# Batch 0 of a linear-attention kernel: value scaling on GpSimd, numerator scaled in PSUM and divided on VectorE, in a reshuffled order

## The chip, the core and the metric

The kernel runs on one core of a Trainium2 chip. A core has five engines that run side by side, each with its own queue of instructions that it takes strictly in order: PE (TensorE, matmuls, results only into PSUM), DVE (VectorE), ACT (ScalarE), POOL (GpSimd, works on SBUF alone in this kernel) and SP (SyncE, which issues DMAs). Semaphores let an instruction wait for another engine. The metric is the device time of one execution in microseconds (us). The kernel before took 360.67 us, the median of three runs from 360.47 to 360.85.

## The reference

```python
# q, k, v: (8 batches, 8 heads, 576 tokens, 64), w_phi: (64, 128)
def phi(x):
    proj = x @ w_phi
    proj = proj - max(abs(proj), axis=-1)
    return concatenate([exp(proj), exp(-proj)], axis=-1)   # 256 features
q_p, k_p = phi(q), phi(k)
kv  = einsum('bhsf,bhsd->bhfd', k_p, v);  z = sum over s of k_p
num = einsum('bhsf,bhfd->bhsd', q_p, kv); den = einsum('bhsf,bhf->bhs', q_p, z) + 1e-6
x = (num / den) as (4608 tokens, 512)
out = (relu(x @ w_gate) * (x @ w_val)) @ w_out             # 512 -> 1536 -> 512
```

## The kernel before, in words

There are two halves: the attention of eight batches, and the feed-forward network (FFN) on their 4608 tokens. Each batch gives 512 tokens in four blocks of 128 (`i` = 0 to 3), and the last 64 tokens of two batches are handled together. FFN work of earlier batches stands between the steps of later ones, so that PE always has something to do, except at the start, where there is no earlier batch.

The order of everything is written out by hand in the string `ORDER`. Each word is one step: a name, its arguments, the PSUM banks after a colon, the SBUF buffers after an `@`. The words are emitted one after the other, and each engine gets its own instructions in that order. Nothing else sets the order; waits come from the data and from the reuse of banks and buffers. The steps that matter here, with their arguments (batch, head group `j` or `g`, block `i`, sign `s`):

- `zz.n` (L455): n matmuls on zeros, which fill PE's time at the start. `kf`, `kg`, `kh` (L645, L654): transpose the first keys. `k3` (L668): projects keys. `wd` (L431): turns `w_phi` into bf16 as soon as its DMA has landed.
- `ke` (ACT L688), `kx` (DVE L696): exponential of the projected keys, and their largest absolute value. `kk` (ACT L705): the factor `ek` per token that undoes the maximum. `kp` (ACT L716): the same, but into PSUM.
- `vs` (POOL L745): v times `ek`, one sign of a head group each; `vo` (POOL L757): the column of `ek` that makes the denominator; `vq` (POOL L773): the same for the leftover 64 tokens. For head group 0 (two heads) of batch 0, and its leftover tokens, DVE does this from PSUM instead: `vd` (L726), `vp` (L735), `vz` (L678).
- `kv` (PE L794): the sum over tokens, for head groups of 2, 3 and 3 heads; each needs its `vs` and the leftover tokens' `vr`. `kc` on ACT or `kd` on DVE (L805) copies it out.
- `qb` (PE L840), `qe` (ACT L869), `qx` (DVE L877), `qy`, `qz`, `qu`, `qw`: the same for q, ending in a scale `cq` for the negative sign.
- `nu` (PE L917): both signs' numerators, side by side in a bank. `nt` (DVE L938) scales the negative sign into `t`, `nv` (DVE L948) adds the positive one into `u`, `nr` (DVE L956) takes the reciprocal of the denominator, `nx` (POOL L960) divides into `xu`.
- `xp`, `xa` (PE L997, ACT L1011): transpose `xu` of batch 0, which `pv` and `pg` (PE L1224), batch 0's part of the FFN input, then read. Later batches use `xt`, a DMA.
- `lk`, `lq`, `lm`, `wl` (POOL) and `lw`, `lv` (SP): loads, where POOL and SP issue the DMAs. `fv`, `fg`, `fi`, `fo`, `fw`: FFN matmuls. `va` (ACT L1112) or `vb` (DVE L1115) copies a value tile out of PSUM, `ga` (DVE L1118) multiplies it in. `ps` (POOL L1337): sums that some `fw` matmuls read.

Of the kernel before, what the change touches and what calls it, by code (L numbers as in the profile page):

```python
# [16 lines left out]
ms.0 lf lm.0.0 ms.4@vr0 ms.6 id lk.0.2 lk.0.0 wq ms.3@vr1 if ms.5 zz.15:0 kf.0:1 ms.9 kf.1:2 zz.6:3  # L17
wd kh.0:1@kT0 sl k3.1.0:45 ke.0.1.0.0:4@kp0 w1:6 kg.1:2 kx.0.1.1:5@mk0 kx.0.1.0:4 wa:6 zz.2:7
k3.1.1:01 ke.0.1.3.0:1 lm.0.1 kx.0.1.2:0 zz.3:3 k0.2:2 lq.0.1 ke.0.1.3.1:1 k1.2:2@kT1 ke.0.1.0.1:4
zz.3:7 k0.0:6 ke.0.1.2.1:0 ke.0.1.1.1:5 k3.2.1:37 ke.0.1.2.0:0 kx.0.1.3:1 ms.2 lw.0.0 lw.0.1  # L20
k1.0:6@kT2 zz.5:4 k3.0.1:21 kk.0.1.0@ek0 k3.0.0:04 ke.0.1.1.0:5 ke.0.0.3.0:1@kp1 q0.1:5 lq.0.0
kx.0.2.3:7@mk1 kx.0.2.2:3 kk.0.1.1 ke.0.2.2.0:3@kp2 kx.0.0.0:0@mk2 kx.0.0.2:2 lv.0.1 ke.0.2.2.1:3
ke.0.0.1.1:4 kx.0.0.3:1 q1.1:5@qT0 ke.0.0.1.0:4 ke.0.0.3.1:1 lv.0.0 zz.6:6 q0.0:6 kx.0.0.1:4 wl.0.1
zz.4:3 k3.2.0:31 lv.0.2 ke.0.2.3.0:7 ke.0.0.2.1:2 ke.0.0.0.1:0 q1.0:6@qT1 ke.0.2.3.1:7 kx.0.2.1:1
zz.1:5 qb.1.1:5 zz.3:4 qb.0.1:4 kx.0.2.0:3 ke.0.0.0.0:0 zz.2:7 qb.0.0:0 qx.0.0.1:4 ke.0.0.2.0:2
zz.1:6 qb.1.0:2 qx.0.1.1:5 zz.7:7 qy.0.1:6 kp.0.0.0:0 ke.0.2.0.0:3 lk.1.3 kk.0.2.1@ek1 kp.0.0.1:0
kk.0.2.0 ke.0.2.1.1:1 vo.1@vs0 qx.0.1.0:2 qe.0.0.1.0:4@qp0 ke.0.2.0.1:3 qe.0.0.1.1:4 lq.1.2
qe.0.1.0.0:2@qp1 qe.0.1.0.1:2 vs.0.1.0 qz.0.1:6@my0 zz.4:7 qb.0.3:7 qx.0.0.0:0 zz.2:6 qy.0.0:3
vd.0.0.0:0@vs1 qz.0.0:3@my1 vs.0.1.1 qe.0.1.1.1:5 vp.0:0 qu.0.1@mz0 ke.0.2.1.0:1 qe.0.1.1.0:5 wl.0.0
vz.0:0 qb.0.2:6 zz.2:4 qb.1.3:3 zz.2:4 qb.1.2:2 vd.0.0.1:0 qu.0.0@mz1 vz.1:0 qe.0.1.3.0:3@qp2  # L30
vo.2@vs2 qw.0.0@cq0 qx.0.0.3:7 qx.0.0.2:6 qe.0.0.0.0:0 vs.0.2.1 zz.7:4 kv.0.0:1 qx.0.1.3:3 lw.1.1
vs.0.2.0 kc.0.0:1@kv0 kt.1.1@kT3 qe.0.0.0.1:0 kv.0.2:5 kv.0.1:4 qe.0.0.2.1:6@qp3 lm.1.1 kc.0.2:5
wl.1.1 kc.0.1:4 nu.0.0.0:1 nt.0.0.0:1@t0 zz.1:0 nu.0.0.2:5 qw.0.1 qx.0.1.2:2 qe.0.0.2.0:6
qe.0.1.3.1:3 nu.0.0.1:0 nv.0.0.0:1@u0 zz.2:4 nu.0.1.2:4 lv.1.2 nu.0.1.0:6 qe.0.1.2.1:2 nt.0.0.1:0@t1
lm.1.0 nt.0.0.2:5@t2 qy.0.2:1 nv.0.0.1:0 qe.0.0.3.0:7 nv.0.0.2:5 nt.0.1.0:6@t3 zz.2:3 nu.0.1.1:3
qy.0.3:0 nr.0.0@r0 qe.0.1.2.0:2 qz.0.2:1@my2 nv.0.1.0:6@u1 qz.0.3:0@my0 qu.0.2@mz2 zz.5:5
kr.1.1:1265 qe.0.0.3.1:7 nt.0.1.2:4@t0 nt.0.1.1:3@t1 qw.0.2 wl.1.0 nu.0.2.2:0 nx.0.0@xu0 nv.0.1.2:4
xp.0.0:7 nv.0.1.1:3 nt.0.2.2:0@t2 ke.1.1.3.1:5@kp3 nr.0.1@r1 nu.0.2.1:4 xa.0.0:7 nt.0.2.1:4@t3
nu.0.2.0:3 ke.1.1.0.1:1 nt.0.2.0:3@t0 qu.0.3@mz1 ke.1.1.0.0:1 pv.1.0:7 nv.0.2.1:4@u2 nv.0.2.2:0
nv.0.2.0:3 nu.0.3.1:4 qw.0.3 ke.1.1.1.0:2 nx.0.1@xu1 kx.1.1.0:1@mk3 xp.0.1:0 pa.1.0:7@val0  # L40
# [246 lines left out]
def kernel(  # L287
# [700 lines left out]
    def xT_cols(b, i):  # L988
        return xT(b)[:, :, P * i : P * (i + 1)]
# [488 lines left out]
```

## Time and profile before

| | |
|---|---|
| median of the runs | 360.67 us |
| the profiled execution itself | 360.87 us |
| span of its instructions | 359.1 us |
| busy: PE, POOL, DVE, ACT | 352.9, 325.6, 312.9, 235.8 us |

The span runs from the first to the last instruction; 1.77 us of the execution's 360.87 lie outside of it. Matmuls are pipelined, so the end of one lies after the start of the next; what PE spends on a step is best read from the starts. A row of a timeline has start, length, engine, line, operation, output and inputs, how many instructions were merged, and in brackets how long the engine had been idle and who released it. A row of the groups by form ends in the summed busy time, the mean of one in ns, and the idle time before them.

### The profile page before, as it was taken

How to read it: one execution, taken by the hardware profiler on the slowest of the kernel's cores; microseconds unless marked ns; L12 is line 12 of the kernel's file. 1: busy time of each engine (PE TensorE's matmuls, PEld its weight loads, DVE VectorE, ACT ScalarE, POOL GpSimd, SP SyncE). 2: the span in 40 equal slices, each digit the busy share in tenths (PEclk: the TensorE clock that was granted, in tenths of full speed). 3: DMA queues.
4: the chain of work that ended last, by engine and by line, in shares of the span. 5: the costliest groups of instructions: out<-in, count | busy, mean ns of one | idle time of the engine just before them, and what ended most of it. 6: DMA issues, size and time to landing. Idle time of an engine off the chain costs nothing.

```text
span 359.1 us, 10076 instructions
## 1 busy us (share of the span) xinstructions
PE 352.9 (98%) x3876; PEld 222.2 (62%) x3876; DVE 312.9 (87%) x721; ACT 235.8 (66%) x564; POOL 325.6 (91%) x393
## 2 busy tenths in 40 slices
PE   8999999999999999999999999999999999999996
PEld 6678966445575656765576546666656566444684
DVE  5999999989999999999997999999898853898744
ACT  3999996986698869786897269656861424454310
POOL 8674988999999999976999589989999999999994
PEclk9999999999999999999999999999999999999999
DMA  7999999990947494369215980778300221600017
GB/s 124 257 198 204 164 199 159 180 164 7 178 68 157 53 157 95 68 127 135 58 39 105 158 136 2 176 107 103 62 0 16 45 59 25 227 0 2 0 31 206
DMA packets 90770, 38.16 MB, mean 106 GB/s; under 512 B 64226, under 2 KB 86370, under 8 KB 90722
## 3 DMA queue, kind: packets, MB, share of 16 engines
q0 software_dynamic: 33504, 15.03, 32.5%
q1 hardware_dynamic: 56754, 21.83, 27.7%
q10 hardware_dynamic: 464, 0.66, 0.8%
q8 instruction: 30, 0.49, 0.6%
q14 instruction: 18, 0.15, 0.1%
HBM read 37.81 MB, written 9.44 MB: 132 GB/s over the span
## 4 chain that ended last, share of the span: by engine, by line
PE 85%; DVE 8%; ACT 2%; DMA 2%; issue 1%; POOL 1%; SPq 0%; DVEq 0%
PE bank L1097 35%; PE bank L1361 18%; PE bank L1194 10%; PE bank L794 5%; PE bank L1224 4%; PE bank L917 3%; PE bank L592 2%; PE bank L854 2%; PE bank L1256 2%; ACT kp L688 2%; DMA w64f<-in_w_phi_dram 2%; DVE t L938 1%; DVE u L948 1%; DVE h L1118 1%; DVE mk L696 1%
## 5 line engine op out<-in xcount | busy, mean ns | idle before, releaser
L688 ACT ACTIVATE kp<-bank 128x384 bf16<-128x384 f32 x192 | 84.2, 513 | 16.6 <-DVE mk L696 7.4
L1097 PE MATMUL bank<-xTs,wv 128*128 128x512 bf16 x304 | 75.7, 379 | 0.0
L1097 PE MATMUL bank<-xTs,wg 128*128 128x512 bf16 x304 | 74.6, 379 | 0.0
L869 ACT ACTIVATE qp<-bank 128x512 bf16<-128x512 f32 x128 | 69.9, 627 | 6.5 <-PE bank L854 4.2
L1118 DVE SCALAR_TENSOR_TENSOR h<-bank,val 128x512 bf16<-128x512 f32 x90 | 60.5, 680 | 6.7 <-PE bank L1097 4.5
L1112 ACT CAST val<-bank 128x512 bf16<-128x512 f32 x59 | 35.1, 594 | 33.4 <-PE bank L1097 30.4
L745 POOL TENSOR_TENSOR vs<-vn,ek 128x780 bf16<-128x780 f32 (+2 forms) x40 | 53.8, 1366 | 0.8 <-ACT ek L705 0.4
L696 DVE TENSOR_REDUCE mk<-bank 128x3 f32<-128x384 f32 x96 | 49.1, 542 | 0.2
L960 POOL TENSOR_TENSOR xu<-u,r 128x512 bf16<-128x512 f32 x36 | 37.4, 1045 | 11.6 <-DVE r L956 11.5
L1361 PEld LDWEIGHTS <-h 128*128 128x128 bf16 x432 | 41.1, 98 | 10.0 <-issue 2.6
L1097 PEld LDWEIGHTS <-wg 128*128 128x128 bf16 x304 | 27.8, 98 | 30.2 <-issue 1.3
L1097 PEld LDWEIGHTS <-wv 128*128 128x128 bf16 x304 | 27.6, 98 | 27.3 <-issue 0.9
L877 DVE TRANSPOSE_TENSOR_REDUCE maxq<-bank 128x16 f32<-128x512 f32 x56 | 36.9, 690 | 0.1
L948 DVE TENSOR_TENSOR u<-bank,t 128x195 f32<-128x195 f32 (+1 forms) x108 | 32.9, 327 | 1.8 <-POOL xu L960 0.9
L1361 PE MATMUL bank<-wo,h 128*128 128x256 bf16 x260 | 32.5, 273 | 0.0
L1337 POOL TENSOR_TENSOR vs<-h 128x256 bf16<-128x256 bf16 x42 | 28.0, 671 | 3.7 <-DVE h L1118 3.6
L938 DVE TENSOR_TENSOR t<-bank,cq 128x195 f32<-128x195 f32 (+1 forms) x96 | 29.6, 326 | 1.9 <-PE bank L917 1.2
L917 PEld LDWEIGHTS <-qp 128*128 128x128 bf16 x512 | 23.1, 98 | 10.2 <-issue 0.5
L1337 POOL TENSOR_TENSOR h<-h,vs 128x256 bf16<-128x256 bf16 x44 | 28.6, 676 | 0.0
L1337 POOL TENSOR_TENSOR vs<-vs,h 128x256 bf16<-128x256 bf16 x42 | 28.0, 672 | 0.6
L1337 POOL TENSOR_TENSOR h<-h 128x256 bf16<-128x256 bf16 x42 | 27.9, 674 | 0.3
L917 PE MATMUL bank<-kv,qp 128*128 128x65 bf16 x512 | 26.0, 193 | 0.2 <-ACT kv L805 0.2
(156 smaller groups left out, 686.0 us busy)
## 6 DMA issues: line engine op xcount, KB each, us to landing
vn<-in_v_dram SPq DMA_DIRECT2D x24, 256.0 KB, 4.3
out_dram<-xTs SPq DMA_DIRECT2D x17, 256.0 KB, 3.0
kn<-in_k_dram POOLq DMA_DIRECT2D x7, 512.0 KB, 8.1
qn<-in_q_dram POOLq DMA_DIRECT2D x7, 512.0 KB, 8.0
out_dram<-obp SPq DMA_DIRECT2D x14, 256.0 KB, 2.6
wv<-in_moe_w_val_dram POOLq DMA_DIRECT2D x3, 512.0 KB, 9.4
wg<-in_moe_w_gate_dram POOLq DMA_DIRECT2D x3, 512.0 KB, 8.8
wo<-in_moe_w_out_dram POOLq DMA_DIRECT2D x3, 512.0 KB, 8.3
```

The source lines that it names most:

```text
L688: nc.scalar.activation(kp_of(3 * b + j)[:, i, s].rearrange("p n f -> p (n f)"), bank[bk[0]][:, 0 : 3 * F], AF.Exp, scale=(1.0, -1.0)[s],)
L696: nc.vector.tensor_reduce(mk_of(3 * b + j)[:, :, i], bank[bk[0]][:, 0 : 3 * F].rearrange("p (n f) -> p n f", f=F), axis=AX.X, op=ALU.max, ...
L745: nc.gpsimd.tensor_tensor(vs_of(3 * b + j)[:, s, 0:n].rearrange("p n i e -> p (n i) e")[:, :, 0:e], src[:, lo:hi].rearrange("p h i e -> p ...
L869: nc.scalar.activation(qp_of(4 * b + i)[:, s, 4 * hq : 4 * hq + 4].rearrange("p h m -> p (h m)"), bank[bk[0]], AF.Exp, scale=(1.0, -1.0)[s],)
L877: nc.vector.tensor_reduce((maxq0[:, i] if b == 0 else maxq)[:, :, i, 4 * hq : 4 * hq + 4].rearrange("p t h -> p h t"), bank[bk[0]].rearran ...
L917: nc.tensor.matmul(bank[bk[0]][:, E * n : E * (n + 1)], lhsT=qp_of(4 * b + i)[:, s, h, :], rhs=kv_of(b)[:, h, s, 0:E],)
L948: nc.vector.tensor_tensor(u_of(serial(b, i))[:, lo:hi], parts(bk, n)[:, :, 0], t_of(3 * serial(b, i) + g)[:, 0:n], op=ALU.add,)
L960: eng.tensor_tensor(xu_of(n).rearrange("p (h d) -> p h d", d=D), u_of(n)[:, :, 0:D], r_of(n).to_broadcast([P, H, D]), op=ALU.mult,)
L1097: nc.tensor.matmul(bank[bk[0]], lhsT=w[:, dc, P * f : P * f + P], rhs=xT(g)[:, dc, :], start=(dc == 0), stop=(dc == NDC - 1),)
L1118: nc.vector.scalar_tensor_tensor(h2_of(g, f), bank[bk[0]], 0.0, val_of(NFC * g + f), op0=ALU.max, op1=ALU.mult)
L1337: eng.tensor_tensor(sum_of(g, n, j), a, b, op=op)
L1361: nc.tensor.matmul(bank[bk[0]][:, col : col + HN], lhsT=x[:, P * u : P * (u + 1)], rhs=w, start=(n in (1, 5, 6) and u == us[0] and j == 0) ...
```

## The change

In batch 0, and only there, two pieces of arithmetic move:

- The scaling of v of head group 0 and of the leftover tokens goes from DVE to POOL: two `kp`, two `vd`, one `vp` and two `vz` are gone, and two `kk`, two `vs`, one `vo` and two `vq` are new. POOL now scales all v.
- The numerator is made in halves of four heads. `bu` with s = 1 puts the negative sign into a bank; `bt` (DVE) scales it there, in PSUM; `bu` with s = 0 adds the positive sign onto it; `br` (DVE) takes the reciprocal of the denominators, and `bx` (DVE) divides into `xu`. 12 `nu`, 12 `nt`, 12 `nv`, 4 `nr` and 4 `nx` (POOL) are gone; 16 `bu`, 8 `bt`, 8 `br` and 8 `bx` are new.

Besides, single copies change engine: of the value tiles, 13 go from DVE to ACT and 8 from ACT to DVE; of the `kv` copies five go from ACT to DVE and one back; one transposed block goes from DVE to ACT and one output block from ACT to DVE. And the whole of `ORDER` is shuffled in small steps. PE has 64 matmuls of the numerator before and after, and 85 matmuls on zeros.

```diff
+    HALVES = ((0, 4), (4, 8))
+    def do_bu(bk, b, i, g, s):
+        lo, hi = HALVES[g]
+        for h in range(lo, hi):
+            n = h - lo
+            nc.tensor.matmul(
+                bank[bk[0]][:, E * n : E * (n + 1)],
+                lhsT=qp_of(4 * b + i)[:, s, h, :],
+                rhs=kv_of(b)[:, h, s, 0:E],
+                start=(s == 1 and h == lo),
+                stop=(h == hi - 1),
+                skip_group_check=(s == 0),
+            )
+    def part(bk, g):
+        lo, hi = HALVES[g]
+        return bank[bk[0]][:, 0 : E * (hi - lo)].rearrange("p (h e) -> p h e", e=E)
+    def do_bt(bk, b, i, g):
+        lo, hi = HALVES[g]
+        nc.vector.tensor_tensor(
+            part(bk, g),
+            part(bk, g),
+            scales(b, i)[:, lo:hi][:, :, None].to_broadcast([P, hi - lo, E]),
+            op=ALU.mult,
+        )
+    def do_br(bk, b, i, g):
+        lo, hi = HALVES[g]
+        nc.vector.reciprocal(r_of(serial(b, i))[:, lo:hi], part(bk, g)[:, :, D : D + 1])
+    def do_bx(bk, b, i, g):
+        n, (lo, hi) = serial(b, i), HALVES[g]
+        nc.vector.tensor_tensor(
+            xu_of(n).rearrange("p (h d) -> p h d", d=D)[:, lo:hi],
+            part(bk, g)[:, :, 0:D],
+            r_of(n)[:, lo:hi].to_broadcast([P, hi - lo, D]),
+            op=ALU.mult,
+        )
...
 ORDER = """
-ms.0 lf lm.0.0 ms.4@vr0 ms.6 id lk.0.2 lk.0.0 wq ms.3@vr1 if ms.5 zz.15:0 kf.0:1 ms.9 kf.1:2 zz.6:3
-wd kh.0:1@kT0 sl k3.1.0:45 ke.0.1.0.0:4@kp0 w1:6 kg.1:2 kx.0.1.1:5@mk0 kx.0.1.0:4 wa:6 zz.2:7
...
+ms.0 lf lm.0.0 ms.4@vr0 ms.6 id lk.0.2 lk.0.0 wq ms.3@vr1 if ms.5 zz.15:0 kf.0:1 kf.1:2 zz.2:3
+zz.5:4 sl kg.1:2@kT0 kh.0:1 zz.6:5 wd k3.1.0:67 kx.0.1.1:7@mk0 k3.1.1:03 zz.3:1 kx.0.1.2:0
```

Three places show what the new order does to single engines. The first is PE and ACT at the very start, in the lines of `ORDER` above: ahead of the first key projection `k3.1.0` stood `zz.6`, and now stand `zz.2`, `zz.5` and `zz.6`, thirteen matmuls on zeros where six were. ACT's first exponential was `ke.0.1.0.0`, which reads what `k3.1.0` wrote; it is now `ke.0.1.3.0`, which reads what `k3.1.1` writes. On ACT the two `kk.0.1` stood behind 7 and 9 of batch 0's `ke` and are now both behind 12 `ke` and `wa`.

The second place is POOL's queue before the first `kv`, first in the kernel before. `vs_97` and `vs_99` are the scaled v of head groups 1 and 2 (12 is 3 heads by 4), `kn`, `qn` the loads of batch 1's k and q, `wv` and `wg` thirds of the FFN's weights.

```order
L464 DMA kn_71<-in_k_dram 128x8x256
L757 CAST vs_97<-ek_91 128x24
L496 DMA qn_73<-in_q_dram 128x8x256
L745 TENSOR_TENSOR vs_97<-vn_75,ek_91 128x12x64 x2
L558 DMA wv<-in_moe_w_val_dram 128x4x512
L757 CAST vs_99<-ek_92 128x24
L745 TENSOR_TENSOR vs_99<-vn_75,ek_92 128x12x64 x2
```

And the same stretch of POOL's queue after the change, where `vs_98` is head group 0 and `vr_103` the leftover tokens:

```order
L465 DMA kn_71<-in_k_dram 128x8x256
L746 TENSOR_TENSOR vs_97<-vn_75,ek_91 128x12x64 x2
L497 DMA qn_73<-in_q_dram 128x8x256
L746 TENSOR_TENSOR vs_98<-vn_75,ek_92 128x8x64
L758 CAST vs_98<-ek_92 128x2x8
L746 TENSOR_TENSOR vs_98<-vn_75,ek_92 128x8x64
L774 TENSOR_TENSOR vr_103<-vm_76,ek_92 64x8x65
L746 TENSOR_TENSOR vs_99<-vn_75,ek_93 128x12x64
L758 CAST vs_97<-ek_91 128x24
L774 TENSOR_TENSOR vr_103<-vm_76,ek_92 64x8x65
L758 CAST vs_99<-ek_93 128x24
L746 TENSOR_TENSOR vs_99<-vn_75,ek_93 128x12x64
```

Five instructions for head group 0 and the leftover tokens now stand among those of groups 1 and 2, and the load of `wv`, which stood between `vs_97` and `vs_99`, stands behind all of them.

The third place is DVE at batch 0's first numerators, in the kernel before (`my` and `h` belong to q's maxima):

```order
L938 TENSOR_TENSOR t_123<-bank_64,cq_115 128x130
L877 TENSOR_REDUCE h_152<-bank_65 128x4x4
L948 TENSOR_TENSOR u_127<-bank_64,t_123 128x130
L938 TENSOR_TENSOR t_124<-bank_63,cq_115 128x195
L938 TENSOR_TENSOR t_125<-bank_68,cq_115 128x195
L948 TENSOR_TENSOR u_127<-bank_63,t_124 128x195
L948 TENSOR_TENSOR u_127<-bank_68,t_125 128x195
L938 TENSOR_TENSOR t_126<-bank_69,cq_115 128x130
L956 RECIPROCAL r_130<-u_127 128x8
```

And after the change, where the copy of batch 0's first `kv` and the transpose of batch 1's q stand ahead of them:

```order
L806 CAST kv_104<-bank_70 128x4x65
L904 STREAM_TRANSPOSE mz_121<-my_119 128x32
L904 STREAM_TRANSPOSE mz_122<-my_117 128x32
L846 STREAM_TRANSPOSE qT_109<-qn_73 128x4x4x32
L1008 TENSOR_TENSOR bank_67<-bank_67,cq_115 128x260
L1008 TENSOR_TENSOR bank_66<-bank_66,cq_115 128x260
L1017 RECIPROCAL r_130<-bank_67 128x4
L1021 TENSOR_TENSOR xu_133<-bank_67,r_130 128x256
L1017 RECIPROCAL r_130<-bank_66 128x4
L1008 TENSOR_TENSOR bank_69<-bank_69,cq_115 128x260
L1021 TENSOR_TENSOR xu_133<-bank_66,r_130 128x256
```

A block needs seven DVE instructions and one on POOL before, and six DVE instructions after, which wait for PE between the scaling and the reciprocal.

More of the change, by code (lines that the diff above doesn't have):

```diff
@@ L23 @@
[L23 to L28, printed above, removed]
@@ new lines @@
+nu.3.3.0:3 fg.2.5:4 ke.4.1.3.1:5 ke.4.1.1.1:6 ps.2.2.4 nr.3.0@r1 ga.2.6:0@hs12 nt.3.3.0:3@t1
+ke.4.1.2.1:2 ga.2.5:4@hs15 nv.3.3.0:3 ps.2.1.0 ps.2.2.0 nr.3.3@r0 kr.4.2:7156 nu.3.2.0:2
+nt.3.2.0:2@t3 ke.4.2.2.0:5@kp0 ke.4.2.3.0:6 ke.4.2.3.1:6 ke.4.2.1.1:1 ke.4.2.2.1:5 mw.1@cm1
+ke.4.2.1.0:1 fg.2.11:0 fv.2.8:4 fg.2.8:3 kx.4.2.0:7@mk1 ga.2.11:0@hs3 kx.4.2.3:6 ke.4.2.0.1:7
+va.2.8:4@val2 kx.4.2.1:1 kx.4.2.2:5 ps.2.3.0 lv.4.3 nv.3.2.0:2@u0 nu.3.2.2:0 nt.3.2.2:0@t0
+ga.2.8:3@hs4 fw.2.1:6 nu.3.2.1:1 nv.3.2.2:0 nt.3.2.1:1@t2 nv.3.2.1:1 kk.4.1.1@ek1 ke.4.2.0.0:7
@@ L1077, in do_mn, with do_bm @@
                     )
+    def do_bm(bk, p, g, s):
+        lo, hi = HALVES[g]
+        for h in range(lo, hi):
+            n = h - lo
+            for bb in range(2):
+                nc.tensor.matmul(
+                    bank[bk[0]][SM * bb : SM * (bb + 1), E * n : E * (n + 1)],
+                    lhsT=qr_of(p)[:, s, h, 2 * bb : 2 * bb + 2, :].rearrange("p i t -> p (i t)"),
+                    rhs=kv_of(2 * p + bb)[:, h, s, 0:E],
+                    start=(s == 1 and h == lo),
+                    stop=(h == hi - 1),
+                    skip_group_check=(s == 0),
+                )
     h2_at = {f: f for f in range(NFC)}
@@ L1364, in do_fw @@
                     rhs=w,
-                    start=(n in (1, 5, 6) and u == us[0] and j == 0),
+                    start=(n in firsts and u == us[0] and j == 0),
                     stop=(u == us[-1] and j == HK - 1),
-                    skip_group_check=(n in (2, 3, 4, 7)),
+                    skip_group_check=(n not in firsts),
                 )
```

544 lines of the change are left out of this document (286 added, 258 removed).

## The prediction, made before the changed kernel had run

> **What bounds the kernel now.** I read the page's busy times first, then the busy time by stretches, to see where PE, the engine that never rests, does rest.
>
> ```profile
> span 359.1 us, 10076 instructions
> PE 352.9 (98%) x3876; PEld 222.2 (62%) x3876; DVE 312.9 (87%) x721; ACT 235.8 (66%) x564; POOL 325.6 (91%) x393
> ...
> 7.10:21.10 14.00, 13.77 (x133) 8.43 (x132) 13.77 (x32) 13.56 (x39) 11.15 (x13) 1.00 1.28 229
> 21.10:28.60 7.50, 7.11 (x169) 5.97 (x168) 7.44 (x25) 7.26 (x19) 3.95 (x6) 1.00 1.28 197
> 28.60:355.50 326.90, 326.07 (x3551) 203.53 (x3550) 288.64 (x657) 213.26 (x508) 304.49 (x363) 1.00 0.57 98
> ```
>
> The columns of a stretch are length, then busy PE, weight loads, DVE, ACT and POOL. From 28.6 to 355.5 us PE is busy 326.07 of 326.90: it is the bound there, and since the matmuls after the change are as many, of the same shapes, that stretch can only shift or gain and lose small waits. Before 28.6 PE looks busy too, but the chain of waits and the same stretches for the matmuls on zeros tell otherwise: they are the filler (8.48 and 1.83 us of the first two rows' PE time), and ACT and DVE run all the time.
>
> ```profile
> 7.10:21.10 14.00, 8.48 (x54) 4.33 (x54) 1.00 1.28 229
> 21.10:28.60 7.50, 1.83 (x11) 1.01 (x10) 1.00 1.28 197
> 28.60:355.50 326.90, 0.00 (x0) 0.00 (x0) 1.00 0.57 98
> ```
>
> So the time is that of the start, up to the first `pv`, plus PE's work from there. The start decides, and I work it out engine by engine.
>
> **Term 1, ACT starts later.** PE's and ACT's timeline at the beginning (the seven zeros at 16.28 are from later, for their rate):
>
> ```profile
> 4.23 1.49 PE L645 MATMUL bank<-identf,xTm 128*128 128x128 f32 x6
> 5.51 1.49 PE L455 MATMUL bank<-zero 128*128 128x256 bf16 x6
> 7.10 0.34 PE L668 MATMUL bank<-w,kT 64*128 64x128 bf16 x6
> ...
> 16.28 0.94 PE L455 MATMUL bank<-zero 128*128 128x256 bf16 x7
> 17.05 0.27 PE L887 MATMUL bank<-identf,h 128*128 128x128 f32 x1
> ```
> ```profile
> 7.46 0.49 ACT L688 ACTIVATE kp<-bank 128x384 bf16<-128x384 f32 x1 [1.86 <-PE bank L668]
> 7.84 0.37 ACT L428 CAST w<-bank 128x256 bf16<-128x256 f32 x1
> 8.20 2.40 ACT L688 ACTIVATE kp<-bank 128x384 bf16<-128x384 f32 x6
> 10.44 0.26 ACT L705 ACTIVATE ek<-mk 128x12 f32<-128x12 f32 x1
> ```
>
> A zero matmul takes 0.21 us up to about 7 us (six, 1.49 with the last one's tail) and 0.11 later (seven from 16.28 to 17.05). With thirteen in place of six behind 5.51, some seven run to 7.0 at the slow rate and six more take 0.66: `k3.1.0` starts at 7.65, not 7.10. ACT's first `ke` followed its projection's start by 0.36; it now waits for `k3.1.1`, half of that 0.34 later. So ACT starts at 8.2, 0.7 us late. Bounds: 0.2 if the fast rate comes earlier, 1.3 if PE stays slow through all thirteen. A `ke` takes 0.373 on ACT (six from 8.20 to 10.44).
>
> The Trainium skill (TensorE: Matmul & The Clock Gate, "What's actually happening") says that PE's clock is halved until a window of about 3.4 us of activity has passed, and that the window runs freely, so that the number of slow matmuls varies from run to run. The trace agrees with the halving (0.21 against 0.11), and its step at 7 us is one draw; by the rule it could come at another time in the changed kernel, which would take up to 0.5 us off the sum.
>
> **Term 2, POOL becomes the last before `kv`.** POOL's timeline, and the rows by form for what is new on it:
>
> ```profile
> 13.14 0.88 POOL L496 DMA_DIRECT2D qn<-in_q_dram  x1 [1.23 <-PE bank L822]
> 14.03 2.92 POOL L745 TENSOR_TENSOR vs<-vn,ek 128x768 bf16<-128x768 f32 x2
> 16.89 0.81 POOL L558 DMA_DIRECT2D wv<-in_moe_w_val_dram  x1
> 17.70 0.30 POOL L757 CAST vs<-ek 128x24 bf16<-128x24 f32 x1
> 18.13 2.91 POOL L745 TENSOR_TENSOR vs<-vn,ek 128x768 bf16<-128x768 f32 x2
> ```
> ```profile
> L773 POOL TENSOR_TENSOR vr<-vm,ek 64x520 bf16<-64x520 f32 x14 | 14.8, 1059 | 1.7 <-ACT ek L705 0.7 <-POOL h L1337 0.5
> L745 POOL TENSOR_TENSOR vs<-xTs,ek 128x512 bf16<-128x512 f32 x2 | 2.1, 1044 | 0.0
> L757 POOL CAST vs<-ek 128x16 bf16<-128x16 f32 x1 | 0.2, 250 | 0.1
> L726 DVE TENSOR_TENSOR vs<-vn,bank 128x512 bf16<-128x512 f32 x2 | 1.3, 661 | 0.0
> L678 DVE TENSOR_TENSOR vr<-vm,bank 64x520 bf16<-64x520 f32 x2 | 1.4, 677 | 0.0
> ```
>
> DVE is rid of 2 x 0.66 + 2 x 0.68 = 2.7 us. POOL gets 2 x 1.04 + 0.25 + 2 x 1.06 = 4.45 us, where it now has the rest of 7.5 us free but not before `kv`. Its first `vs` waits for `kk.0.1.1`, behind 12 `ke` and `wa`: 8.2 + 12 x 0.373 + 0.36 + 0.26 = 13.3. The queue behind it: 2.92 for group 1, 0.88 for the q load, 4.45 for what is new, 2.91 for group 2, 0.60 for two casts, together 11.75, less some 0.04 of overlap at each of ten borders: the last `vs` ends at 24.7. Before, it ended at 18.13 + 2.91 = 21.04, and `kv` began in that moment:
>
> ```profile
> 21.04 0.28 PE L794 MATMUL bank<-vs,kp 128*128 128x65 bf16 x4
> ...
> 23.46 0.29 PE L917 MATMUL bank<-kv,qp 128*128 128x65 bf16 x4
> ...
> 28.67 1.05 PE L1224 MATMUL bank<-xTs,wv 128*128 128x128 bf16 x16 [0.20 <-ACT xTs L1011]
> ```
>
> The 80 matmuls of the three `kv` took 2.42 us, 0.030 each; the last `kv.0.2` needs 30, and the other two fit in before it. It ends at 24.75 + 0.9 = 25.7, against 23.46: 2.2 us late. The DMA issues behind POOL's last `vs` start late as well (term 4).
>
> **Term 3, the way from `kv` to `pv` gets shorter.** Before it went through POOL; the rows that price it and its replacement:
>
> ```profile
> 23.15 1.01 ACT L805 CAST kv<-bank 128x390 bf16<-128x390 f32 x2
> ...
> 28.03 0.59 ACT L1011 COPY xTs<-bank 128x512 bf16<-128x512 bf16 x1 [0.16 <-PE bank L997]
> ```
> ```profile
> L960 POOL TENSOR_TENSOR xu<-u,r 128x512 bf16<-128x512 f32 x36 | 37.4, 1045 | 11.6 <-DVE r L956 11.5
> L948 DVE TENSOR_TENSOR u<-bank,t 128x195 f32<-128x195 f32 x72 | 24.3, 352 | 0.7
> L1216 DVE TENSOR_TENSOR val<-bank,u 128x512 bf16<-128x512 f32 x24 | 15.8, 684 | 4.6 <-PE bank L1194 3.4 <-ACT u L1210 1.2
> L956 DVE RECIPROCAL r<-u 128x8 f32<-128x8 f32 x36 | 6.7, 189 | 0.2
> ```
>
> No row has DVE writing PSUM. By size, `bt` (260) and `bx` (256) lie between 0.352 (195) and 0.684 (512): 0.42 each; the ends are 0.35 and 0.68, and I take 0.42 as the line through them. `br` is taken as 0.19. From the last `kv` at 25.7: `kc` 0.5 to 26.25; two zeros and `bu` 0.45 to 26.7; `bt` to 27.15; `bu` with s = 0 and its tail 0.3 to 27.5; then DVE's queue runs `br`, `bx`, `br`, `bt` and the `bx` that completes the block, 2 x 0.19 + 3 x 0.42 less 0.35 of overlap, to 28.75; `xp` 0.4 and `xa` 0.59 to 29.75, when `pv` may start. From the end of `kv` that is 4.0 us where it was 28.67 - 23.46 = 5.2: 1.2 us won, of 2.2 lost. At 0.68 for `bt` and `bx` the four on that way cost 1.0 more; at 0.35, 0.3 less.
>
> `pv` thus starts 1.1 us late. At that moment the kernel before still had 16 numerator matmuls of batch 0 to do, the order after has 28 behind its `pv.1.0`: 12 x 0.03 = 0.35 more. Terms 1 to 3 together: **+1.4 us**, with PE, which waits in this stretch, paying each of them in full.
>
> **Term 4, the weights.** The first third of `wv` was issued at 16.89; its issue now stands behind POOL's last `vs`, at 24.7. For `wl`'s six loads the source line gives:
>
> ```profile
> DMA to landing us min/median/max: 6.2/9.1/11.3
> ```
>
> It lands between 30.9 and 36.0, and `pv.0.0`, the first to read it, is due at 29.75 + 0.9 + 0.45 = 31.1. So between 0 and 4.9 us of waiting. I take 6.4 and a wait of 0.2, near the lower end, because the q load that POOL issues ahead of it (13.14 before, 13.3 + 2.9 = 16.2 now) has by then been under way for 8.5 us, and had 3.75 us before.
>
> **Term 5, small waits later.** PE waits for POOL twice near the end of batch work:
>
> ```profile
> 292.40 1.48 PE L1361 MATMUL bank<-wo,vs 128*128 128x256 bf16 x12 [0.22 <-POOL vs L1337]
> ...
> 295.39 1.48 PE L1361 MATMUL bank<-kp,vs 128*128 128x256 bf16 x12 [0.20 <-POOL vs L1337]
> ```
>
> The new order has `fi.0.1.5`, `fi.0.3.5` and `fi.0.2.5` ahead of these two `fw`, so POOL's sums are done: -0.4 us. The other stretches have 326.90 - 326.07 = 0.83 us of waits altogether, so nothing larger can be won there.
>
> ```profile
> L1112 ACT CAST val<-bank 128x512 bf16<-128x512 f32 x59 | 35.1, 594 | 33.4 <-PE bank L1097 30.4 <-DVE u L948 1.2 <-DVE h L1118 1.0
> ```
>
> At nothing I cost: five more value copies on ACT (it idles 33.4 us before these), five fewer on DVE, and the `kv` and block copies that change engine, all beside a busy PE; if the cover goes, each costs its 0.5 to 0.7 us once. POOL's four `nx` (4.2 us) go where POOL was idle.
>
> **Sum:** +1.4 + 0.2 - 0.4 = +1.2. Against the profiled execution's 360.87 (span 359.1) that is 362.1; its time is 0.2 above the median of the runs, so against 360.67 I predict 361.9.
>
> **Rivals.**
> - *The short way wins (faster).* If POOL's last `vs` ended by 22.6, for example because the ACT chain ahead of `kk.0.1` is quicker, `kv` would end at 23.5 as before, `pv` start at 27.5, and the kernel gain 1.2 - 0.35 + 0.4: 359.4. It decides at a last `vs` before 23.4. POOL's sum of 11.4 from 13.3 speaks against it, DVE's 2.7 us less for it. Chance 0.14.
> - *Start and later waits cancel (same).* The loss of the start is 1.4 with errors of half a us in each term; with the fast rate earlier, the lower bound of term 1 (-0.5), and the small waits (-0.4) some 0.5 stays: 361.1. Chance 0.22. (The Trainium skill's rule of the free-running window, TensorE: Matmul & The Clock Gate, allows that draw.)
> - *The weights are late (slower still).* With 9.1 to landing, `pv.0.0` waits 2.7 us in place of 0.2: 364.4; half of that is 363.1. For it: the SP queue's loads of v for batch 1, which wait for the last reader of the leftover tokens' v, now POOL's `vq`, fall on the same moment. Chance 0.14.
> - *The forecast:* 0.50, from 361.3 to 362.9.
>
> The range that leaves out 2 in 10: 360.2 to 363.6. What a measurement can tell from no change is about 0.2%, 0.7 us, so faster is below 359.95 and slower above 361.4. Faster 0.14; same 0.22 plus the lowest part of the forecast, 0.24; slower 0.62.
>
> **What would show it.** In the changed kernel's profile: the first `ke` at 8.2; POOL without a break from 13.3 to 24.7; `kv` ending near 25.7; `bt` and `bx` near 0.42 us; the first `pv` near 29.8, with PE idle or on zeros before; `pv.0.0` without a DMA wait; PE busy from there to the end. The prediction is wrong if POOL's queue has gaps or ends before 23.4, if `bt` is dear, or if PE waits anew after 40 us.

## The result, and the profile after

The changed kernel takes 365.63 us, the median of four runs from 364.49 to 366.63, against 360.57 for the kernel before in the same session: 1.0139 times as long (95% interval 1.0108 to 1.0170), 5.1 us slower. The direction was forecast; the size, 1.2 us, was not, and the time lies outside the range.

The profiled execution of the changed kernel is the longest of the four, 366.63 us, 5.76 above the profiled one of before. The busy times of its page:

```profile
PE 354.5 (97%) x3876; PEld 224.5 (62%) x3876; DVE 312.5 (86%) x711; ACT 235.1 (64%) x565; POOL 325.6 (89%) x394
```

They tell nearly nothing: PE has as many matmuls and is busy 1.6 us longer. The busy time by stretches tells more, if both kernels are cut at the same steps. First before, from its first `kv` matmul to its first `pv`, from there to the first matmul of the FFN's output (`wo,h`), and from there to the end:

```profile
21.04:28.67 7.63, 7.17 (x171) 6.03 (x168) 7.57 (x26) 7.39 (x19) 4.08 (x6) 1.00 1.28 198
28.67:57.46 28.79, 28.79 (x501) 23.00 (x501) 28.54 (x67) 28.07 (x72) 22.81 (x27) 1.00 1.19 182
57.46:355.51 298.05, 297.29 (x3056) 180.53 (x3052) 260.03 (x590) 185.12 (x435) 281.61 (x337) 1.00 0.51 90
```

And after, at the same steps:

```profile
22.58:30.75 8.17, 7.25 (x150) 6.38 (x147) 6.43 (x21) 6.73 (x18) 5.51 (x8) 0.79 0.81 134
30.75:62.39 31.64, 30.21 (x518) 24.09 (x518) 29.68 (x69) 27.00 (x69) 20.50 (x24) 1.00 1.18 173
62.39:361.31 298.92, 297.16 (x3052) 180.72 (x3048) 259.75 (x587) 184.76 (x438) 281.05 (x337) 1.00 0.51 90
```

The first `pv` is 2.08 us late (30.75 against 28.67), the second stretch is 2.85 longer, the third 0.87: together 5.80. In the second stretch PE never rested before (28.79 of 28.79) and now rests 31.64 - 30.21 = 1.43. In the first, the granted clock fell to 0.79, and the core's DMA engines moved 134 GB/s where they had moved 198. What PE waited for, summed by releaser:

```profile
PE bank L1279 <- DMA wg<-in_moe_w_gate_dram: 1.2, 1, 1.2
PE bank L456 <- DVE zero L442: 1.1, 1, 1.1
PE bank L888 <- ACT qp L870: 1.0, 1, 1.0
PE bank L1249 <- POOL qT L1224: 0.9, 1, 0.9
PE bank L1417 <- POOL vs L1392: 0.7, 1, 0.7
...
PE bank L1279 <- DMA wv<-in_moe_w_val_dram: 0.3, 1, 0.3
```

L1279 is `pv` and `pg`: batch 0 now waits for weights, which it did not before. POOL's timeline shows where those loads stand; no wait is named in its queue from 12.92 on, and the three loads of weights (the third, of `wg`, at 27.38) come behind the last `vs`:

```profile
12.92 2.90 POOL L746 TENSOR_TENSOR vs<-vn,ek 128x768 bf16<-128x768 f32 x2 [2.78 <-ACT ek L706]
15.77 0.94 POOL L497 DMA_DIRECT2D qn<-in_q_dram  x1
...
22.94 1.48 POOL L746 TENSOR_TENSOR vs<-vn,ek 128x768 bf16<-128x768 f32 x1
24.35 0.82 POOL L559 DMA_DIRECT2D wv<-in_moe_w_val_dram  x1
25.17 0.72 POOL L509 DMA_DIRECT2D km<-in_k_dram  x1
25.89 0.79 POOL L559 DMA_DIRECT2D wg<-in_moe_w_gate_dram  x1
```

PE's timeline shows the two places, and the first `pv` before them:

```profile
26.54 0.28 PE L993 MATMUL bank<-kv,qp 128*128 128x65 bf16 x4
...
30.75 1.05 PE L1279 MATMUL bank<-xTs,wv 128*128 128x128 bf16 x16
...
32.67 1.07 PE L1279 MATMUL bank<-xTs,wv 128*128 128x128 bf16 x16 [0.26 <-DMA wv<-in_moe_w_val_dram]
33.57 0.53 PE L993 MATMUL bank<-kv,qp 128*128 128x65 bf16 x12
33.94 1.95 PE L1279 MATMUL bank<-xTs,wv 128*128 128x128 bf16 x32
37.06 1.07 PE L1279 MATMUL bank<-xTs,wg 128*128 128x128 bf16 x16 [1.17 <-DMA wg<-in_moe_w_gate_dram]
```

The arithmetic itself cost what was taken for it. The groups by form of `bt`, `bx` and `br`:

```profile
L1008 DVE TENSOR_TENSOR bank<-bank,cq 128x260 f32<-128x260 f32 x8 | 3.4, 425 | 0.7 <-PE bank L993 0.5
L1021 DVE TENSOR_TENSOR xu<-bank,r 128x256 bf16<-128x256 f32 x8 | 3.3, 418 | 0.1
L1017 DVE RECIPROCAL r<-bank 128x4 f32<-128x4 f32 x8 | 1.4, 170 | 0.5 <-PE bank L993 0.4
```

### The profile page after: what moved, and what is told of

The parts are those of the page before. It is cut to its first block, busy times and chain, and to the rows that moved or that the text cites. A ratio compares the mean times of both kernels' runs of the same rounds, so it can differ in the third digit from the quotient of the medians.

```text
span 364.9 us, 10055 instructions
## 1 busy us (share of the span) xinstructions
PE 354.5 (97%) x3876; PEld 224.5 (62%) x3876; DVE 312.5 (86%) x711; ACT 235.1 (64%) x565; POOL 325.6 (89%) x394
## 4 chain that ended last, share of the span: by engine, by line
PE 78%; POOL 9%; DMA 8%; SPq 2%; DVE 1%; issue 1%; ACT 0%; POOLq 0%
PE bank L1151 29%; PE bank L1417 18%; PE bank L1249 10%; PE bank L795 4%; POOL vs L746 3%; PE bank L918 3%; PE bank L1279 3%; DMA wg<-in_moe_w_gate_dram 3%; PE bank L1311 3%; DMA vm<-in_v_dram 2%; PE bank L593 2%; PE bank L855 2%; DMA vn<-in_v_dram 2%; POOL vs L1392 2%; POOL h L1392 1%; PE bank L456 1%
## 5 line engine op out<-in xcount | busy, mean ns | idle before, releaser
L1151 PE MATMUL bank<-xTs,wv 128*128 128x512 bf16 x304 | 74.8, 379 | 0.0
L870 ACT ACTIVATE qp<-bank 128x512 bf16<-128x512 f32 x128 | 70.9, 629 | 5.5 <-DVE maxq L878 3.1
L1166 ACT CAST val<-bank 128x512 bf16<-128x512 f32 x64 | 38.1, 601 | 42.3 <-PE bank L1151 27.6
L746 POOL TENSOR_TENSOR vs<-vn,ek 128x780 bf16<-128x780 f32 (+3 forms) x42 | 56.0, 1349 | 4.2 <-ACT ek L706 3.0
L1417 PEld LDWEIGHTS <-h 128*128 128x128 bf16 x432 | 41.6, 98 | 8.9 <-issue 1.3
L961 POOL TENSOR_TENSOR xu<-u,r 128x512 bf16<-128x512 f32 x32 | 33.2, 1043 | 4.5 <-DVE r L957 3.6
L1417 PE MATMUL bank<-wo,h 128*128 128x256 bf16 x260 | 32.5, 273 | 0.0
L949 DVE TENSOR_TENSOR u<-bank,t 128x195 f32<-128x195 f32 (+1 forms) x96 | 29.8, 328 | 1.7
L939 DVE TENSOR_TENSOR t<-bank,cq 128x195 f32<-128x195 f32 (+1 forms) x84 | 25.6, 323 | 1.3 <-PE bank L918 0.8
L918 PEld LDWEIGHTS <-qp 128*128 128x128 bf16 x448 | 20.2, 97 | 9.8 <-DVE kv L806 0.3
L795 PEld LDWEIGHTS <-kp 128*128 128x128 bf16 x640 | 23.2, 101 | 3.2 <-issue 0.4
## 6 DMA issues: line engine op xcount, KB each, us to landing
wg<-in_moe_w_gate_dram POOLq DMA_DIRECT2D x3, 512.0 KB, 11.1
```

The costliest lines, as they stand in the source:

```text
L746: nc.gpsimd.tensor_tensor(vs_of(3 * b + j)[:, s, 0:n].rearrange("p n i e -> p (n i) e")[:, :, 0:e], src[:, lo:hi].rearrange("p h i e -> p ...
L795: nc.tensor.matmul(out_ps[:, h - lo, s, :], lhsT=lhsT, rhs=rhs, start=(at == 0), stop=(at == 2 * n * (C + 1) - 1),)
L870: nc.scalar.activation(qp_of(4 * b + i)[:, s, 4 * hq : 4 * hq + 4].rearrange("p h m -> p (h m)"), bank[bk[0]], AF.Exp, scale=(1.0, -1.0)[s],)
L1151: nc.tensor.matmul(bank[bk[0]], lhsT=w[:, dc, P * f : P * f + P], rhs=xT(g)[:, dc, :], start=(dc == 0), stop=(dc == NDC - 1),)
L1166: nc.scalar.copy(val_of(NFC * g + f), bank[bk[0]])
L1417: nc.tensor.matmul(bank[bk[0]][:, col : col + HN], lhsT=x[:, P * u : P * (u + 1)], rhs=w, start=(n in firsts and u == us[0] and j == 0), s ...
```

## Experiments

The kernels are called e1 to e13, in the order in which they ran. Times are medians; the ratio is against the kernel before, run beside on the same chip. Edits to the changed kernel are words of `ORDER`, as a diff against it.

### The late weights, and the halved clock

Three kernels tell two suspects apart: the first third of `wv` issued early, PE kept busy in its pause ahead of the `kv` (so that its clock stays up), and both.

```diff
 e1, e3: -qe.0.0.1.1:6 wl.0.0 lw.1.1        +qe.0.0.1.1:6 lw.1.1
         -qy.0.1:0 vs.0.1.1@vs0             +qy.0.1:0 wl.0.0 vs.0.1.1@vs0
 e2, e3: -qb.0.3:1 qy.0.0:4                 +qb.0.3:1 zz.8:4 qy.0.0:4
```

> The changed kernel with one step moved: wl.0.0, the issue of the first third of wv, stands ahead of POOL's first vs (in POOL's idle time from 10.1 to 12.9 us) and not behind the last. Theory W (the late weights cost most of what I had not forecast): pv.0.0 no longer waits at 32.7, wg's first third, issued 0.8 us earlier and with one load less ahead of it, lands some 3 us earlier than 37.0, and the time falls by 2 to 2.5 us, to about 363.3. Theory C (PE's halved clock during kv costs it) and theory Q (POOL's long queue alone): no change, within 0.5 us of 365.6.

Measured: 363.45 us, ratio 1.0079 (1.0058 to 1.0100): 2.2 us below the changed kernel. PE's waits in its profile name no weight any more:

```profile
PE bank L888 <- ACT qp L870: 1.0, 1, 1.0
PE bank L615 <- DMA km<-in_k_dram: 0.9, 1, 0.9
PE bank L993 <- DVE bank L1008: 0.4, 1, 0.4
```

The early load itself took 12.9 us to land, in time all the same; the first load of `wg`, issued 0.5 us earlier than in the changed kernel and with one load less ahead of it, took 6.3 us in place of 11.1. The 0.9 us for `km` at 9 us is a new wait.

> The changed kernel with eight more matmuls on zeros (bank 4) ahead of qy.0.0, in the 0.98 us in which PE waits just before kv. Theory C: PE's clock is not halved from 22.9 to 26.3, the three kv take 2.4 us and not 3.9, and the time falls by 1.2 us, to about 364.4. Theory W: the clock stays full too, but pv.0.0 and pg.1.0 wait for weights that land at 32.6 and 37.0 whatever PE does before, so the time stays within 0.4 us of 365.6.

Measured: 365.87 us, ratio 1.0129 (1.0111 to 1.0147). The stretch of the `kv` in the changed kernel, and the same stretch here, of which the columns behind the engines are granted clock, DMA share and GB/s:

```profile
22.00:27.00 5.00, 4.66 (x105) 4.63 (x108) 3.89 (x12) 3.56 (x9) 4.93 (x7) 0.66 0.46 89
```
```profile
22.00:27.00 5.00, 4.43 (x128) 3.98 (x127) 4.55 (x13) 4.79 (x13) 4.93 (x8) 1.00 0.56 100
```

The clock stayed up and the first `pv` came at 28.98 in place of 30.75 (0.45 of that is an earlier first `ke`, see term 1 below), yet the kernel gained nothing, because PE then waited longer for the same loads:

```profile
PE bank L1279 <- DMA wg<-in_moe_w_gate_dram: 1.9, 1, 1.9
PE bank L1249 <- POOL qT L1224: 1.4, 1, 1.4
PE bank L1279 <- DMA wv<-in_moe_w_val_dram: 1.4, 1, 1.4
```

So in the changed kernel it is the landing of the weights that sets the time of this stretch; the halved clock ahead of it is hidden behind them. The clock does not explain e1 either, though it was mostly up there: the one execution of e1 with a mean clock of 0.994, as low as in the changed kernel, took 363.52 us, no more than the others.

> Both edits, the early wv and the eight zeros. If both theories hold, W hides what C costs: the time falls by more than the first edit alone, by 3 to 3.7 us, to about 362.2. If the clock costs nothing, it is that of the first edit, about 363.3.

Measured: 364.26 us, ratio 1.0100 (1.0076 to 1.0123), 2 us above what was expected. The early weights push batch 1's q load back, which stands behind them; its transpose on DVE (`qt.1.0`), which waited 1.14 us for that load, stands ahead of `bt`, and PE waited 1.0 us for `bt` (L1008). In the profiled run that pause was followed by a halved clock in the middle of `pv`:

```profile
30.00:34.00 4.00, 3.84 (x47) 3.74 (x47) 3.16 (x11) 2.83 (x8) 0.00 (x0) 0.57 1.27 208
```

With the weights early, such a halved stretch seems to cost: the two executions of e3 with a mean clock of 0.995 took 364.74 and 364.94 us, the two with 1.0 took 363.78 and 363.37. The latter are no better than e1, so the zeros won nothing that can be told apart.

### One part of the change at a time

First the weights again, from the other side: the kernel before, with nothing changed but the place of that one load.

```diff
 e6 (before): -qe.0.1.1.0:5 wl.0.0 vz.0:0     +qe.0.1.1.0:5 vz.0:0
              -qw.0.2 wl.1.0 nu.0.2.2:0       +qw.0.2 wl.1.0 wl.0.0 nu.0.2.2:0
```

> The kernel before with one load moved: the first third of wv is issued behind the other loads at about 23.2 us in place of 16.9; no arithmetic and no order of any other engine changes. Theory that late weights are what the forecast missed: it lands 8.3 us later, at 31.5, where pv.0.0 was due at 29.96, and PE waits 1.5 us that nothing gives back: 362.0. Rival, the wait is hidden or caught up later: 360.5 to 360.8.

Measured: 369.87 us, ratio 1.0263 (1.0244 to 1.0281), 9.6 us slower, six times what was expected. PE's timeline:

```profile
28.99 0.39 PE L997 MATMUL bank<-ident,xu 128*128 128x128 bf16 x4
36.54 1.89 PE L1224 MATMUL bank<-xTs,wv 128*128 128x128 bf16 x16 [7.16 <-DMA wv<-in_moe_w_val_dram]
```

Issued at 23.63, behind four other loads of POOL and several of SP, the load landed 12.9 us later, not 8.3. The loads ahead of it are the likely reason; no run varied their number alone. After the pause of 7.16 us the sixteen matmuls took 1.89 in place of 1.06. A load that had 3.5 us to spare (landed at 26.5, read at 29.96) thus cost 9.6 us when it lost its place.

Next, the first part of the change in the order of the kernel before: POOL scales all v.

```diff
 e5 (before): -kp.0.0.0:0 kp.0.0.1:0 vd.0.0.0:0@vs1 vd.0.0.1:0 vp.0:0 vz.0:0 vz.1:0
              +kk.0.0.0@ek5 kk.0.0.1 vs.0.0.0@vs1 vs.0.0.1 vo.0 vq.0.0 vq.0.1
```

> The kernel before with the first part of the change alone: POOL scales all v of batch 0, the numerators stay as they were. Theory: POOL gets 4.45 us more ahead of its last vs, which then ends at 21.04 + 4.45 = 25.5; the last kv follows within 0.9, at 26.4 in place of 23.46, and since the numerators still take their long way, pv starts 2.9 us late (31.6): the kernel takes 360.5 + 2.9 = 363.4. The first third of wv is issued only 1.4 us late here (five instructions of POOL ahead of it are now seven), so no weight is waited for. Rival, DVE's relief of 2.7 us shortens the way to kv or to the numerators: +1 at most, 361.5. If the weights decide nothing in this kernel but the time is still above 364.5, the late kv costs more than its delay.

Measured: 365.73 us, ratio 1.0144 (1.0123 to 1.0166), as slow as the whole change, with no weight waited for:

```profile
PE bank L794 <- POOL vs L745: 2.8, 1, 2.8
PE bank L455 <- DVE zero L441: 1.1, 1, 1.1
PE bank L794 <- POOL vr L773: 0.7, 1, 0.7
```

POOL's last `vs` ended at 25.67 (25.5 was expected), but here two of the three `kv`, not one, stand behind it on PE, and after the wait the clock halved: `kv` ended at 27.89, and `pv` began at 33.24, 4.6 us late where 2.9 was expected. DVE's relief gave nothing back: from the end of `kv` to `pv` it took 5.35 us, against 5.2 before. In this order the first part of the change is a loss of itself; no run gave it an order made for it.

The opposite, group 0 and the leftover tokens scaled on DVE, from SBUF, between its `qx`:

```diff
 e4, do_vs: -        nc.gpsimd.tensor_tensor(
            +        (nc.vector if (b, j) == (0, 0) else nc.gpsimd).tensor_tensor(
 e4, ORDER: +qx.0.0.0:1 vs.0.0.1@vs1 vo.0 ... qx.0.0.2:0 vs.0.0.0 qx.0.1.3:3 vq.0.0 vq.0.1
```

> The changed kernel with the scaling of v of head group 0 and of the leftover tokens on DVE again (the same instructions, from SBUF, placed between q's maxima on DVE); POOL's queue is 4.45 us shorter. Theory Q (POOL's queue is the root: it makes kv late and the weights late): POOL's last vs ends near 20 us, the weights are issued there, and the time falls by 4 us or more, to about 361.5. Theory W alone: the weights come 4.4 us earlier, so 2 to 2.5 us, 363.3. A rival: DVE, with 2.7 us more, becomes the last before kv, and only 1 us is won, 364.6.

Measured: 368.02 us, ratio 1.0206 (1.0190 to 1.0222). `vo` and `vq` moved in the same way. POOL's last `vs` ended at 21.9 and no weight was waited for, but DVE, whose two `vr` took 2.37 us, became the last before `kv`:

```profile
PE bank L888 <- DVE h L878: 3.7, 1, 3.7
```

That is the rival's cause, at more than its price (364.6).

Then the second part alone: the kernel before with `bu`, `bt`, `br` and `bx` in the places of `nu`, `nt`, `nv`, `nr` and `nx`.

```diff
 e10 (before): -nu.0.0.0:1 nt.0.0.0:1@t0 zz.1:0 nu.0.0.2:5 ... nu.0.0.1:0 nv.0.0.0:1@u0 ...
               +bu.0.0.0.1:1 bt.0.0.0:1 zz.1:0 bu.0.0.0.0:1 bu.0.0.1.1:5 ... br.0.0.0:1@r0 bx.0.0.0:1@xu0 ...
```

> The kernel before with the second part of the change alone: batch 0's numerators in halves, scaled in PSUM and divided on DVE, each in the place of the old ones; v is scaled on DVE and POOL as before, and the loads stay where they were. Theory (term 3): the way from kv to the first pv is 1.2 us shorter and at most 0.35 of it is paid back: 359.6 against 360.5. Rival: bt waits behind other work in DVE's full queue, or pv was bound by something else: 360.2 to 361.

Measured: 364.12 us, ratio 1.0097 (1.0072 to 1.0122): slower, not faster. From the end of `kv` (22.81) to the first `pv` (30.33) it took 7.5 us, against 5.2 before and 4.2 in the changed kernel, and PE's waits say why:

```profile
PE bank L993 <- DVE bank L1008: 2.5, 4, 0.9
...
PE bank L993 <- ACT kv L806: 0.5, 1, 0.5
PE bank L1279 <- DVE xu L1021: 0.5, 1, 0.5
```

In one bank the second sign can only be added when the first has been scaled, so PE and DVE take turns. Where the order leaves work between (the changed kernel), the way is short; in the old places, it is longer than the old arithmetic.

### What is left when the start is mended

Two kernels take away the small waits, with the weights early in the second. The third adds the zeros and moves batch 1's `qt` behind the last `bx`.

```diff
 e7, e8, e9: -xs.0.1.0 fi.0.1.5:0 ys.6:5 ... fw.6.2:5 fi.0.2.5:6     +xs.0.1.0 ys.6:5 ... fw.6.2:5 fi.0.1.5:0 fi.0.2.5:6
 e8, e9:     wl.0.0 as in e1
 e8:         qt.1.0@qT2 behind bx.0.0.1:3
 e9:         zz.8:4 as in e2; qt.1.0@qT2 behind bx.0.3.0:6
```

> The changed kernel with fi.0.1.5 moved behind fw.6.2, so that the late transposed q, which it waited for, is asked for one step later. Theory: the 0.9 us that PE waited at 297 us are gone and the kernel gains 0.6 to 0.9 us against the changed one (365.7): about 364.9. Rival: the wait turns up at the next matmul that needs the same block, and nothing is gained, 365.7.

Measured: 365.24 us, ratio 1.0137 (1.0118 to 1.0155). The wait at 297 us went from 0.9 to 0.5; that is too little to be told from no change.

> The changed kernel with the first third of wv ahead of POOL's vs, the transpose of batch 1's q behind the first bx on DVE (it waited for a load there), and fi.0.1.5 behind fw.6.2. Theory: the weights' 2.2 us, 0.6 of the q load and 0.6 of the late wait come off 365.7: 362.3, what terms 1 to 3 with a sum of 1.4 leave (361.9). If terms 1 to 3 were themselves too small, it stays above 363.

Measured: 364.53 us, ratio 1.0113 (1.0096 to 1.0130). That is 2.2 us above what was expected. The move of `qt` was a bad one: it takes DVE 1.09 us, and PE now waited 0.93 for the `bt` behind it, with a halved clock in `pv` after it.

> The changed kernel with four moves: the first third of wv ahead of POOL's vs, eight more matmuls on zeros before qy.0.0 (PE idled 0.98 us there), batch 1's transposed q behind the last bx of batch 0 on DVE, where it takes nobody's turn, and fi.0.1.5 behind fw.6.2. Theory: with no weight waited for, no halved clock and no q load in the way of bt, only terms 1 to 3 are left; with zeros at that place pv started at 28.98, 0.3 us late, and 0.35 of numerators remain: 360.5 + 0.65, about 361.2. Rival: if it stays above 362.5, a part of the loss lies in the new order elsewhere, and not at the start.

Measured: 364.11 us, ratio 1.0095 (1.0073 to 1.0117), the outcome of its rival. No weight is waited for and the clock is 0.999 to 1.0 in all six runs, and 3.5 us are still lost.

So three kernels joined the two orders at about 60 us, where both have done the same steps but four (banks and buffers renamed to fit).

```diff
 e11: order before, up to mc.0 and kv.1.0   then   order after, from nu.1.1.1
 e12: order after, up to mc.0               then   order before, from me.0.2.0
 e13: as e12, with the start of e9
```

> Two orders joined at about 60 us, where both have done the same steps but four: the kernel before up to there, with its own batch 0, and the order of the changed kernel from there on (banks and buffers renamed to fit). It has the reshuffled order without either part of the change. Theory that term 5 had the wrong sign: the later waits of the changed kernel (PE's unexplained time after 63 us was 1.3 us above that of before) come with this order, so 361.5 to 361.9 against 360.5. Rival, those waits are late loads that the late start pushes along: 360.5. The forecast's term 5 was 0.4 faster: 360.1.

Measured: 361.50 us over 12 runs, ratio 1.0021 (1.0005 to 1.0038). The new order after 60 us costs 0.2 to 1.4 us of itself; the gain of 0.4 that was forecast is outside of that.

> The other join: the changed kernel up to about 60 us, and the order of the kernel before from there on. Theory: the start costs terms 1 to 3 and the late weights, 1.4 + 2.2, with what the halved clock adds: 364.1 to 364.5, and 1.3 below the changed kernel. Rival, the later order costs nothing of itself: 365.6.

Measured: 366.14 us, ratio 1.0145 (1.0118 to 1.0172): no gain against the changed kernel, where 364.1 to 364.5 was expected. Its stretches, cut as above:

```profile
29.36:61.46 32.10, 30.03 (x509) 24.02 (x513) 29.32 (x67) 27.27 (x70) 19.61 (x23) 1.00 1.19 178
61.46:360.05 298.59, 295.06 (x3015) 180.66 (x3052) 260.06 (x590) 185.00 (x436) 281.60 (x337) 1.00 0.52 90
```

Its `pv` began 1.39 us earlier than in the changed kernel's profile, and the stretch behind it became 0.46 longer, with 1.7 us of waiting for `wg` in place of 1.2: the weights take a part of what the start wins ahead of them. The profiles do not settle the rest, since the one of e12 (365.55) lies below the median of its kernel and the one of the changed kernel (366.63) above.

> The start of the experiment without waits (weights early, eight more zeros, the transposed q out of the way) joined with the order of the kernel before from about 60 us on. If the late order costs 1.3 and the start of that experiment 2.2, this is 362.8; if all that was left there was the start, 364.

Measured: 363.51 us, ratio 1.0079 (1.0053 to 1.0105), between the two: 0.6 below the same start with the new order, which the intervals do not part.

```profile
29.93:60.40 30.47, 29.91 (x509) 24.05 (x513) 29.43 (x68) 27.38 (x70) 19.62 (x23) 1.00 1.13 168
60.40:358.02 297.62, 294.98 (x3015) 180.81 (x3052) 260.11 (x590) 185.11 (x436) 281.71 (x337) 1.00 0.52 90
```

Its loss of 2.5 us in the profile lies all ahead of 60.4: 1.26 until the first `pv`, 1.68 from there to the output matmuls, and the rest of the kernel is 0.43 shorter. No version beat the kernel before.

## Why the prediction was right or wrong

*Term 1* (ACT 0.7 us later) was right as a mean and poor for any one run. The thirteen zeros took 1.58 to 2.31 us in ten profiles with the new start and the six took 0.82 to 1.49 in five with the old; the first `ke` began at 7.09 to 8.35, mean 7.77, against 6.71 to 7.46, mean 7.15: 0.62 apart. In the changed kernel's profile it began at 7.76. It does not always pass on. Between e2 and e9 it did: the first `ke` began at 7.31 and 8.35, the first `pv` at 28.98 and 30.04. But in e1, e4 and e12, with a first `ke` at 7.26, 7.20 and 7.09, POOL's first `vs` began only at 13.22, 13.23 and 12.86, against 12.92 in the changed kernel and 12.47 in e2; in e4 and e12 it waited for the load of v, and in e1 PE had waited for `km` before. An early start of ACT wins nothing when a load is due after it. The Trainium skill (TensorE: Matmul & The Clock Gate, "What's actually happening") says that the window runs freely and the step comes at another place in each run; these draws agree.

*Term 2* was right for POOL: from 12.92 to 24.42, 11.5 us of queue where 11.4 was worked out. `kv` ended at 26.54, not 25.7, because PE's clock was halved from 22.9 to 26.3, while the `kv` ran: where it stayed up, in e2, `kv` ended 0.81 us after POOL's last `vs` (0.9 was taken), and in the changed kernel 2.12 after. The sum held no term for that; e2 shows that, behind late weights, it cost nothing in the end.

*Term 3* was right in its pieces (0.425 and 0.418 where 0.42 was taken, 0.17 where 0.19) and in its way, 26.54 to 30.75, 4.2 us where 4.0 was taken. What it missed is that this is a property of the order and not of the arithmetic (e10).

*Term 4* is the step that failed most. It was taken at 0.2 us, from bounds of 0 to 4.9. Early weights give 2.2 us back (e1). The 0.2 does not follow from the working either: an issue at 24.7 and 6.4 us to landing make 31.1, the due time itself. The issue time was right (24.35 for 24.7). The time to landing was not: 6.4 was taken, as if the queue ahead were shorter than before, while this load took 8.3, the median of the three loads of `wv`:

```profile
DMA to landing us min/median/max: 6.0/8.3/9.3
```

That PE waited only 0.26 us for it, near the 0.2, is luck: the late `kv` had put off the due time too. And, more, the term looked at the first load alone. The loads of `wg` behind it had moved from 21.73 to 25.89 as well; the first of them landed 11.1 us later, and it held PE four times as long (1.2 against 0.3 us). The rival on late weights had the mechanism right, named 363.1 to 364.4, still below the 365.6 that was measured, and was given 0.14.

*Term 5* had the wrong sign: 0.4 of gain forecast, 0.2 to 1.4 us of loss measured (e11). It looked at two waits of the old order and not for new ones; in the changed kernel PE waits 0.9 for `fi.0.1.5` (L1249) and 0.7 for POOL's sums (L1417). In e11's profile only 0.3 of the first is left, so these two are not all of e11's loss; where the rest lies was not taken apart.

*Added up* on medians, the weights are 2.2 (e1) and the later order about 0.7 (e11). The other 2.2 of the 5.1 stand against the 1.4 of terms 1 to 3; e13, which has neither the late weights nor the new later order, loses 2.6 (1.9 to 3.8). So terms 1 to 3 together were short too, by about 1 us, twice the reserve of 0.5 that the forecast had for them. Where it lies, the times from the first `pv` to the first `pg`, and from there to the output matmuls, tell, first in the changed kernel and then in e1:

```profile
30.75:37.06 6.31, 4.88 (x88) 4.51 (x88) 6.08 (x17) 4.10 (x11) 0.00 (x0) 1.00 1.28 202
37.06:62.39 25.33, 25.33 (x430) 19.58 (x431) 23.60 (x53) 22.90 (x59) 20.50 (x24) 1.00 1.15 165
```
```profile
29.91:34.58 4.67, 4.56 (x92) 4.46 (x89) 4.64 (x17) 2.97 (x8) 0.00 (x0) 1.00 1.26 205
34.58:59.90 25.32, 25.32 (x432) 19.57 (x430) 24.65 (x55) 23.97 (x61) 20.43 (x24) 1.00 1.14 167
```

Behind the first `pg` the two are alike; ahead of it the late weights cost 1.64 us. But e1, which waits for no weight, still takes 29.99 us from `pv` to the output matmuls, against 28.79 before: 1.20 more, where the forecast had 0.35 for the numerators. The twelve numerators are there, and four of batch 1 (0.12) that came later before; the other 0.7 us are spread over pauses too small for the profile's rows, and no run took them apart, so their cause stays open. The sentence that PE's work behind `pv` "can only shift or gain and lose small waits" left no room for them. In e13 this stretch is 1.68 longer; the 0.5 beyond e1's come with a wait for DVE's `h` (41.28 to 41.89), which only e9 and e13 show, the two with batch 1's `qt` moved behind the last `bx`.

## What to carry to other kernels

A load that is issued from a queue with arithmetic in it moves with that arithmetic, and all the loads behind it move too: price each one by its own due time, and do not take a short time to landing: loads of 512 KB of weights took 5.5 to 14.2 us in these profiles. When a wait is removed upstream of such a load, ask first whether the load sets the time; two of the experiments (e2, e12) brought `pv` forward by over 1 us in their profiles and won nothing on medians. Moving work to an engine with free time asks that this time lie ahead of the due point: POOL had 9% of the span free, but 2.85 us from 7.1 to 21.1, and 4.45 were added there.

## What the runs showed of the hardware

PE's clock fell to half after short pauses. In the changed kernel PE had been idle for 0.98 us at most, with pauses of up to 0.2 us ahead of it, and was busy for 2.15 of the 3.4 us before the drop; the mean clock of 22 to 27 us was 0.66, which is half rate for 3.4 of 5 us. All four runs had a mean clock of 0.994 or 0.995. In the seven profiles that show a halved stretch ahead of the very end it lasts 3.4 us, but for e6, where it lasts three times that. With eight more matmuls on zeros in the pause it stayed at 1.00. The same pause of 0.98 us stands in the profiles of e1, e7, e8 and e12, and only in e7 did a halved clock follow it; e1 had mean clocks of 0.998, 1.0, 0.994 and 1.0 over its four runs. So the pause alone does not decide, and no run shows what else does. The Trainium skill (TensorE: Matmul & The Clock Gate, "What's actually happening") gives a whole idle window of about 3.4 us as the condition for the drop; here 3.4 us with PE busy for 2.15 of them were enough.

A move of one load cost more than any move of arithmetic in this study: 9.6 us for the one 512 KB third of `wv`, whose issue came 6.7 us later and whose landing came 10 us later (36.5 against 26.5).
